# Moving the fold of three batches out of the recurrent part and reordering the last units of a fused mLSTM, soft-MoE and MLP kernel

## The chip, the core and the metric

The kernel runs on one core of a Trainium2 chip. The metric is the device time in microseconds; the median over runs is compared. The engines are TensorE (PE; its weight loads are listed apart as PEld), VectorE (DVE), ScalarE (ACT), GpSimd (POOL) and SyncE (SP), whose queue issues the transfers.

## What is computed

Three layers in a row: a matrix LSTM with exponential gates over 4 x 8 heads of 768 steps and width 40, a soft mixture of 8 experts with 4 slots each, and an MLP with a squared ReLU.

```python
def _attn_ref(q, k, v, i_gate, f_gate, o_gate):
    ...
        m_new = np.maximum(f_gate[:, :, t] + m, i_gate[:, :, t])
        C = f_stab[:, :, None, None] * C + i_stab[:, :, None, None] * np.einsum('bhd,bhe->bhde', vt, kt)
        n = f_stab[:, :, None] * n + i_stab[:, :, None] * kt
        ...
        y[:, :, t] = o * h_tilde / denom

def _moe_ref(x, phi, w1, w2):
    logits = x @ phi
    d = softmax of logits over the tokens; c = softmax of logits over the slots
    slot_input = d.T @ x
    for e in range(E):
        h = np.maximum(slot_input[e] @ w1[e], 0.0)
        slot_out[e] = h @ w2[e]
    return c @ slot_out

def _moe2_ref(x, w_in, w_out):
    g = np.maximum(x @ w_in, 0.0) ** 2
    return g @ w_out
```

(The softmax lines are shortened to words.)

## The kernel before

The recurrence is cut into chunks of 128 steps and groups of three heads (the last group has two): 11 groups of 6 chunks are the `units` of the main loop. A unit has products for the decay mask (`e_mb`, L440), for the scores q k (`e_st`, L471), for the state's update (`e_u`, L499), for what the earlier chunks give (`e_inter`, L544) and for the chunk itself (`e_av`, L559). VectorE multiplies scores and mask to `p` (`e_pm`, L483), updates the state (`e_uc`: `cu` at L518), and GpSimd masks it (`e_mask`, `cbd` at L534); `e_num` (tmp at L581, num at L588) and `fin` or `fin_last` (L611 to L653) make the outputs x in SBUF.

The order on each engine is the order in which the code is written: nothing reschedules it. Work for the mixture is put between the units by generators: `filler` is called once or twice in a unit with a string of tags, and each tag (P for transposes on TensorE, N, D and n for VectorE, A for ScalarE, G and g for GpSimd, Q for the logits) lets waiting generators take a step. One of them is `merge`, which brings the three finished batches' slot sums xs3 to one common maximum and folds them into one group of 32 rows: the product `xs3 x cb3` at L798, three products of two passes each, in the bank ps_lt, copied to xs4[96:128] at L804. Another is `merge_tr`, which transposes the outputs of the last batch (`moe_kt`, L675, kt = 0 and 1) and takes the logits (L684).

Behind the loop stands straight code for the last batch. The third part of the outputs is transposed (kt2, L1054) and copied (L1056), its logits are taken, and the maximum follows: nmx (L1066), mxr (L1070), a product for the row maximum (L1072). `tr_el` transposes the exponentials, and VectorE copies them to `en` (L1080, L1081). The slot sums `xx` (L1096) are combined with the folded batches (L1109 to L1114) to the experts' inputs. Then come the experts' layers: `ffn_up(0)` and `ffn_up(1)` (L1148), `relu` (L1153, scaled by rt128, L1172 and L1173), the transposes `ffn_tr` (L1200) and `ffn_down` (L1219). Weights of the experts stream in meanwhile.

In between stand two side tasks. `cbuild(tg)` prepares the combine weights of 512 tokens: its first step casts and subtracts on VectorE (chl, L1015 and L1016), its second transposes four times on TensorE into a bank of the tag o or m (L1022), its third copies on ScalarE (cst, L1027); `cgo(a, b)` takes the next step of a and of b. `wo_narrow(f)` rebuilds a part of the MLP's output weights: two passes on ScalarE (L140, L144) and two on VectorE (L148, L152). `warm(n)` puts n bf16 products in a place where TensorE waits (L197).

PSUM has two banks each of the tags mb, st and o, one of m, and ps_lt; a tag's banks are taken in turn, so a writer waits for whatever still reads the bank's former tile. From 186 us on the MLP runs over the tokens (L1344 and L1416).

Of the kernel before, what the change touches and what calls it, by code (L numbers as in the profile page):

```python
# [20 lines left out]
END = "PADNngG"  # L21
# [22 lines left out]
def kernel(  # L44
# [446 lines left out]
    def e_u(g, c):  # L491
        nh = groups[g][1]
        nd, nv = nh * D, nh * DV
        n = units.index((g, c)) + 2
        t = bank("st")
        if n < NU:
            stk[units[n]] = t
        u = t[:, 384:512]
        nc.tensor.matmul(  # L499
            u[0:nd, 0:nv],  # L500
            lhsT=kin[g][:, c].rearrange("p n d -> p (n d)"),
            rhs=wvs.pop((g, c)).rearrange("p n d -> p (n d)"),
            start=True,
            stop=True,
        )
        us[g, c] = u

    def e_uc(g, c):
        nh = groups[g][1]
        nd, nv = nh * D, nh * DV  # L510
        uv = us.pop((g, c))[0:nd, 0:nv].rearrange("p (n d) -> p n d", d=DV)
        hv = hm[0:nd, 0:nh].unsqueeze(2).to_broadcast([nd, nh, DV])
        cb = cb01[g, c % 2] if g < 2 else wk.tile([120, nh, DV], F32, tag="cbd", name="cbd", bufs=2)
        if c == 0:
            nc.vector.tensor_tensor(out=cb[0:nd], in0=uv, in1=hv, op=ALU.mult)
        else:
            cu = wk.tile([120, nh, DV], F32, tag="cu", name="cu", bufs=1)
            nc.vector.scalar_tensor_tensor(  # L518
                out=cu[0:nd],
                in0=cbds[g, c - 1][0:nd],  # L520
                scalar=dec120[0:nd, g, c : c + 1],
                in1=uv,
                op0=ALU.mult,
                op1=ALU.add,
            )
            masks.append((cb[0:nd], cu[0:nd], hv))
        cbds[g, c] = cb
# [235 lines left out]
    def merge():  # L763
# [30 lines left out]
        yield "P"  # L794
        t = ltb
        nc.tensor.matmul(t[:, DM : DM + B1], lhsT=sel4f[0:96], rhs=tt3, start=True, stop=True)
        for b in range(B1):
            nc.tensor.matmul(  # L798
                t[96:128, 0:DM], lhsT=cb3[:, b, :], rhs=xs3[:, b, :], start=(b == 0), stop=(b == B1 - 1)
            )  # L800
        yield "N"
        nc.vector.tensor_reduce(out=se4[96:128], in_=t[96:128, DM : DM + B1], axis=AX.X, op=ALU.add)
        yield "A"
        nc.scalar.copy(xs4[96:128], t[96:128, 0:DM])  # L804

    def merge_tr():
        yield from moe_kt(B - 1, 0)
        yield from moe_kt(B - 1, 1)
        yield "Q", {"merge"}
        logits(range(2))  # L810

# [74 lines left out]
    for i, (g, c) in enumerate(units):  # L886
# [73 lines left out]
        elif i > 1 and nm:  # L960
            finish(nm)
            g1, c1 = units[i - 2]
            if c1 == NC - 1:
                add(fin(g1), ("fin", g1), [("sig", b) for b in batches(g1)])
        elif g == NG - 1 and c > 1:
            f1 = fin(g, c - 3, c - 1)
            if c == 3:
                add(f1, ("fin", g), [("sig", B1)])
            else:
                for _ in range(3):  # L970
                    next(f1)
        if i >= QI:
            advance("Q", 1)
        filler(END, i >= LI, i < 20)
    xf = xb[B - 2].rearrange("p c d -> p (c d)")
    hsb = xf[:, 0:FF]
    sT01 = xf[:, FF : FF + 64 * NE].rearrange("p (k w) -> p k w", k=2)
# [7 lines left out]
    while fillers:  # L985
        advance("W")
        filler("QPNADngG")
    while w2s:
        ld_w2(*w2s.pop(0))
    pl.close()  # L990
# [43 lines left out]
    def cgo(*tgs):  # L1034
        for tg in tgs:
            next(cbs[tg], None)
# [5 lines left out]
    for n in (4, 5):  # L1042
        ld_w2(w2p[n], *w2o[2 + n])
    load_wo(wo0, 0, 4)
    dumt = bank("mb")
    cgo(0, 1)
    warm(WT[6], dumt)
    x3 = xb[B1]
    k0, kn = KT[2]
    xT = xTs[2]  # L1050
    for blk in (range(0, 4), range(4, 6)):
        t = bank("o")
        for n, c in enumerate(blk):
            nc.tensor.transpose(t[0:kn, 128 * n : 128 * n + 128], x3[:, c, k0 : k0 + kn], ident)  # L1054
        w = 128 * len(blk)
        nc.scalar.copy(xT[0:kn, 128 * blk[0] : 128 * blk[0] + w], t[0:kn, 0:w])  # L1056
        warm(WT[5], dumt)
    logits([2])
    load_wo(xTw[:, 0 : SLOT // 2], 6, 2)
    cgo(0)  # L1060
    warm(WT[0], dumt)
    el_ = mp.tile([128, 2, TQ], F32, tag="el", name="el")
    el = el_[0:96]
    en = mp.tile([128, 2, 2, 96], F32, tag="en", name="en")
# [7 lines left out]
    nc.tensor.matmul(tm[:, 0:4], lhsT=sel4f, rhs=mxr, start=True, stop=True)  # L1072
    rm = ca.tile([128, 1], F32, name="rm")
    nc.vector.tensor_reduce(out=rm, in_=tm[:, 0:4], axis=AX.X, op=ALU.max, negate=True)
    warm(WT[1], dumt)

    def tr_el(m):
        t = bank("mb" if m == 0 else "o")
# [9 lines left out]
    nc.vector.tensor_scalar(out=comb, in0=selF, scalar1=es, scalar2=None, op0=ALU.mult)  # L1088
    tt = ca.tile([128, 1], F32, name="tt")
    nc.vector.tensor_tensor(out=tt, in0=es, in1=se4, op=ALU.mult)  # L1090
    cgo(0, 1, 2)
    warm(WT[2], dumt)
    xx = bank("st")
    for u in range(2):
        for r in range(NQ):
# [6 lines left out]
            )  # L1102
    nc.scalar.copy(xs4[0:96, 0:128], xx[0:96, 0:128])
    nc.vector.tensor_copy(xs4[0:96, 128:DM], xx[0:96, 128:DM])
    cgo(1, 2, 3)
    warm(WT[3], dumt)
    t = bank("st")
    for kt in range(2):
        nc.tensor.matmul(  # L1109
# [16 lines left out]
    load_wo(x3.rearrange("p c d -> p (c d)")[:, 0 : SLOT // 2], 4, 2)  # L1126
    for n in (6, 7):
        ld_w2(w2p[n], *w2o[2 + n])
    cgo(3)
    warm(WT[4], dumt)  # L1130
    NP = NE // 2
    ys = {}

# [25 lines left out]
    for n in range(4):  # L1159
        for r in range(2):  # L1160
            nc.vector.tensor_copy(
                repm[32 * n : 32 * n + 32, 64 + 128 * n + 32 * r : 96 + 128 * n + 32 * r],
                ident[32 * n : 32 * n + 32, 32 * n : 32 * n + 32],
            )
    finish(wo_narrow(0, *par_t))
    cgo(2, 3)
    for h in range(2):
        nc.gpsimd.memset(hT[:, 4 * h : 4 * h + 4], 0.0)
    for n in range(6):
# [37 lines left out]
        )  # L1207

    ffn_up(1, range(0, 3))
    ffn_tr(0)  # L1210
    ffn_up(1, range(3, 5))
    relu(1)
    so = bank("st")
# [14 lines left out]
    next(n4)  # L1228
    next(n4)
    ffn_down(0)  # L1230
    ffn_tr(1)
    next(cl)
    finish(n4)
    finish(cl)
# [283 lines left out]
```

## Time and profile before

| | us |
|---|---|
| median of 3 runs | 387.26 (387.14 to 388.26) |
| the profiled execution | 386.97 |
| its span | 385.2 |
| TensorE busy | 374.2 |
| VectorE busy | 264.1 |
| ScalarE busy | 254.0 |
| GpSimd busy | 102.9 |

Times in the views count from the start of the span. The recurrence with its fillers takes until about 152 us, the mixture's last part until 182, the MLP the rest. The view of stages lists for each stretch the busy time of every engine, the granted clock (PEclk, 1.00 is the upper level) and the mean share of the DMA engines. The chain is followed back from the last instruction: each piece is what held up the end at that time. The timelines list groups of one engine, line and tile, with the idle time ahead of them and what ended it.

### The profile page before, as it was taken

The numbers are of one execution on the slowest core, as the hardware profiler recorded it, in microseconds if no ns is written. First come the engines' busy times: TensorE is split into PE (matmuls) and PEld (weight loads), VectorE is DVE, ScalarE is ACT, GpSimd is POOL, SyncE is SP. The second block draws the span as 40 slices with busy tenths as digits, with TensorE's granted clock in tenths as the row PEclk, the third lists the DMA queues.
The fourth block names the chain that finished last, engine by engine and source line by source line (L and its number), as shares of the span: only waits on it lengthen the run. The fifth ranks groups of instructions, "written<-read, shape, count | busy, mean of one in ns | idle before, by whom it ended". The sixth has DMA issues, their size and how long they took to land.

```text
span 385.2 us, 9124 instructions
## 1 busy us (share of the span) xinstructions
PE 374.2 (97%) x3420; PEld 333.4 (87%) x3420; DVE 264.1 (69%) x602; ACT 254.0 (66%) x579; POOL 102.9 (27%) x208
## 2 busy tenths in 40 slices
PE   8899999999899999999999999999999999999996
PEld 6789998889879886435699899999999999999996
DVE  7868889878988577738688865555555555555551
ACT  7798776569656752544697976676676667657652
POOL 4665976766677546000000000000000000000000
PEclk9999999999999999999999999999999999999999
DMA  5886897899969786999000010020010001002001
GB/s 174 280 299 207 282 314 235 260 325 344 305 185 386 212 324 195 361 378 381 2 3 0 2 68 3 0 70 0 3 66 4 1 2 68 2 1 70 1 2 68
DMA packets 19541, 56.62 MB, mean 147 GB/s; under 512 B 2481, under 2 KB 7561, under 8 KB 19113
## 3 DMA queue, kind: packets, MB, share of 16 engines
q1 hardware_dynamic: 19497, 56.04, 42.7%
q8 instruction: 27, 0.44, 0.5%
q14 instruction: 17, 0.14, 0.1%
HBM read 52.10 MB, written 3.93 MB: 145 GB/s over the span
## 4 chain that ended last, share of the span: by engine, by line
PE 79%; DVE 8%; POOL 5%; ACT 3%; issue 3%; SPq 1%; DMA 0%; POOLq 0%; DVEq 0%; ACTq 0%
PE ps_mb L1416 18%; PE ps_st L1416 17%; PE ps_lt L1416 9%; PE ps_st L471 7%; PE ps_o L1344 4%; PE ps_o L559 4%; PE ps_o L544 3%; PE ps_st L1219 2%; DVE p L483 2%; PE ps_m L1344 2%; PE ps_st L499 2%; PE ps_lt L684 2%; POOL w L461 2%; PE ps_mb L440 1%; DVE x L631 1%
## 5 line engine op out<-in xcount | busy, mean ns | idle before, releaser
L1367 DVE CAST hi<-ring 128x512 fp32r<-128x512 f32 x93 | 39.7, 427 | 61.2 <-ACT ring L1366 53.0
L1368 DVE TENSOR_TENSOR lo<-ring,hi 128x512 fp32r<-128x512 f32 x96 | 66.5, 692 | 9.8
L454 ACT ACTIVATE w<-ps_mb,qt 128x128 f32<-128x128 f32 x192 | 56.5, 367 | 17.2 <-PE ps_mb L440 10.1
L1349 ACT ACTIVATE ring<-ps_o 128x512 f32<-128x512 f32 x64 | 38.3, 598 | 34.2 <-PE ps_o L1344 34.2
L1366 ACT ACTIVATE ring<-ring 128x512 f32<-128x512 f32 x93 | 58.8, 633 | 3.0
L471 PE MATMUL ps_st<-par 120*128 120x128 f32 (+1 forms) x384 | 56.9, 284 | 0.1
L1416 PE MATMUL ps_mb<-wohlh,hi 128*128 128x320 f32 x160 | 49.5, 310 | 0.0
L1416 PE MATMUL ps_mb<-wohlh,lo 128*128 128x320 f32 x160 | 49.4, 310 | 0.0
L1416 PE MATMUL ps_mb<-wohll,hi 128*128 128x320 f32 x160 | 49.3, 309 | 0.0
L471 PEld LDWEIGHTS ps_st<-par 120*128 120x128 f32 (+1 forms) x384 | 47.9, 192 | 0.3 <-issue 0.3
L1416 PE MATMUL ps_st<-wohll,hi 128*128 128x320 f32 x144 | 44.7, 310 | 0.0
L1416 PE MATMUL ps_st<-wohlh,hi 128*128 128x320 f32 x144 | 44.7, 310 | 0.0
L1416 PE MATMUL ps_st<-wohlh,lo 128*128 128x320 f32 x144 | 44.6, 310 | 0.0
L461 POOL TENSOR_SCALAR_AFFINE_SELECT w<-w 128x384 f32<-128x384 f32 (+1 forms) x66 | 37.1, 562 | 17.8 <-ACT w L454 12.1
L483 DVE TENSOR_TENSOR p<-ps_st,w 128x384 f32<-128x384 f32 (+1 forms) x66 | 35.5, 538 | 4.7 <-POOL w L461 3.7
L1416 PEld LDWEIGHTS ps_mb<-wohll,hi 128*128 128x128 f32 x160 | 30.0, 188 | 1.4
L1349 ACT ACTIVATE ring<-ps_m 128x512 f32<-128x512 f32 x32 | 19.1, 598 | 18.4 <-PE ps_m L1344 18.4
L1416 PEld LDWEIGHTS ps_mb<-wohlh,hi 128*128 128x128 f32 x160 | 30.1, 188 | 0.0
L1416 PEld LDWEIGHTS ps_mb<-wohlh,lo 128*128 128x128 f32 x160 | 30.1, 188 | 0.0
L559 PE MATMUL ps_o<-par,p 128*64 128x41 f32 x768 | 29.0, 232 | 0.0
L1416 PEld LDWEIGHTS ps_st<-wohll,hi 128*128 128x128 f32 x144 | 27.1, 188 | 2.0 <-issue 0.6
L559 PEld LDWEIGHTS ps_o<-par,p 128*64 128x64 f32 x768 | 25.1, 138 | 4.0 <-issue 0.2
(275 smaller groups left out, 772.0 us busy)
## 6 DMA issues: line engine op xcount, KB each, us to landing
ring<-in_w_dram SPq DMA_DIRECT2D x22, 640.0 KB
stage<-in_w_in_dram SPq DMA_DIRECT2D x10, 512.0 KB
par<-in_w_dram SPq DMA_DIRECT2D x6, 640.0 KB
out_dram<-ring SPq DMA_DIRECT2D x24, 160.0 KB
par<-in_v_s_dram SPq DMA_DIRECT2D x9, 369.0 KB
par<-in_k_s_dram SPq DMA_DIRECT2D x9, 360.0 KB
x<-in_o_gate_dram SPq DMA_DIRECT2D x9, 320.0 KB
par<-in_k_t_dram SPq DMA_DIRECT2D x23, 120.0 KB
```

What stands on the lines that cost most here:

```text
L454: nc.scalar.activation(w[:, j, :], mb[:, 128 * j : 128 * j + 128], AF.Exp, bias=qt3[:, c, h0 + j : h0 + j + 1])
L461: nc.gpsimd.affine_select(out=w, in_=w, pattern=[[0, nh], [1, 128]], compare_op=ALU.is_ge, fill=0.0, base=0, channel_multiplier=-1)
L471: nc.tensor.matmul(st[:, 128 * j : 128 * j + 128], lhsT=kbd[g % 2][0:nd, j, ts_], rhs=qin[g][0:nd, ts_], start=True, stop=True,)
L483: nc.vector.tensor_tensor(out=p, in0=sts.pop((g, c))[:, 0 : nh * 128].rearrange("p (n t) -> p n t", n=nh), in1=ws.pop((g, c)), op=ALU.mult,)
L544: nc.tensor.matmul(pos[g, c // 2][:, o0 : o0 + nv], lhsT=qin[g][0:nd, 128 * c : 128 * c + 128], rhs=cbds[g, c - 1][0:nd], start=True, stop ...
L559: nc.tensor.matmul(po[t0 : t0 + 64, o0 : o0 + DV], lhsT=p[:, j, t0 : t0 + 64], rhs=vin[g][:, c, j, :], start=True, stop=True,)
L1344: nc.tensor.matmul(t, lhsT=gst[n][:, 128 * k : 128 * k + 128], rhs=cst[tg], start=True, stop=True)
L1349: nc.scalar.activation(r, t, AF.Relu)
L1366: nc.scalar.activation(r, r, AF.Square)
L1367: nc.vector.tensor_copy(hi, r)
L1368: eng.tensor_tensor(out=lo, in0=r, in1=hi.bitcast(F32), op=ALU.subtract)
L1416: nc.tensor.matmul(acc[u][:, 0:DM], lhsT=l_[:, 128 * u : 128 * u + 128], rhs=wohl[r_, f // 8][:, f % 8, :], start=(f == 0 and a == 0), sto ...
```

## The change

It does this:

- `merge` no longer folds; a generator `fold` holds the three products, now in a bank of the tag st, and takes them one by one: one behind the kt2 transposes, one behind the logits of kt2, one behind tr_el. The copy to xs4[96:128] follows the last one.
- The keep-warm products of this part (`warm(WT[...])`) go.
- The update products of the last units c = 3 and 4 take a bank of the tag mb rather than sharing a st bank, and for the last three units VectorE both masks and adds (`e_uc`) in place of VectorE and then GpSimd.
- `fin` of the last group comes one unit earlier, and the fillers of the last two units are cut, so that the transposes of kt = 0 and 1 stand behind the last unit's products.
- The second copy of kt2 is VectorE's.
- The steps of `cbuild` are put at other places: chl(0) to chl(3) are each transposed later than before.

```diff
 def e_u(g, c):
-        t = bank("st")
-        if n < NU:
+        t = bank("st" if n < NU - 1 else "mb")
+        if n < NU - 1:
             stk[units[n]] = t
 ...
 def e_uc(g, c):
+            if units.index((g, c)) >= NU - 3:
+                nc.vector.tensor_tensor(out=cu[0:nd], in0=uv, in1=hv, op=ALU.mult)
+                nc.vector.scalar_tensor_tensor(
+                    out=cb[0:nd],
+                    in0=cbds[g, c - 1][0:nd],
+                    scalar=dec120[0:nd, g, c : c + 1],
+                    in1=cu[0:nd],
+                    op0=ALU.mult,
+                    op1=ALU.add,
+                )
+                cbds[g, c] = cb
+                return
 ...
 def merge():
         nc.tensor.matmul(t[:, DM : DM + B1], lhsT=sel4f[0:96], rhs=tt3, start=True, stop=True)
+        folds.append(cb3)
+        yield "N"
+        nc.vector.tensor_reduce(out=se4[96:128], in_=t[96:128, DM : DM + B1], axis=AX.X, op=ALU.add)
+
+    folds = []
+
+    def fold():
+        t = bank("st")
         for b in range(B1):
             nc.tensor.matmul(
-                t[96:128, 0:DM], lhsT=cb3[:, b, :], rhs=xs3[:, b, :], start=(b == 0), stop=(b == B1 - 1)
-            )
-        yield "N"
-        nc.vector.tensor_reduce(out=se4[96:128], in_=t[96:128, DM : DM + B1], axis=AX.X, op=ALU.add)
-        yield "A"
+                t[96:128, 0:DM], lhsT=folds[0][:, b, :], rhs=xs3[:, b, :], start=(b == 0), stop=(b == B1 - 1)
+            )
+            if b < B1 - 1:
+                yield
         nc.scalar.copy(xs4[96:128], t[96:128, 0:DM])
+        yield
 
     def merge_tr():
         yield from moe_kt(B - 1, 0)
-        yield from moe_kt(B - 1, 1)
+        yield from moe_kt(B - 1, 1, ("m", "mb"))
 ...
-        elif g == NG - 1 and c > 1:
-            f1 = fin(g, c - 3, c - 1)
-            if c == 3:
+        if g == NG - 1 and c in (2, 4):
+            finish(nm or ())
+            nm = None
+            f1 = fin(g, c - 2, c)
+            if c == 2:
                 add(f1, ("fin", g), [("sig", B1)])
 ...
-        filler(END, i >= LI, i < 20)
+        filler(END if i < NU - 2 else "ADngG" if i == NU - 2 else "", i >= LI, i < 20)
 ...
+    fd = fold()
 ...
-    dumt = bank("mb")
-    cgo(0, 1)
-    warm(WT[6], dumt)
 ...
-        nc.scalar.copy(xT[0:kn, 128 * blk[0] : 128 * blk[0] + w], t[0:kn, 0:w])
-        warm(WT[5], dumt)
+        (nc.vector.tensor_copy if blk[0] else nc.scalar.copy)(
+            xT[0:kn, 128 * blk[0] : 128 * blk[0] + w], t[0:kn, 0:w]
+        )
+    next(fd)
+    cgo(0)
     logits([2])
     load_wo(xTw[:, 0 : SLOT // 2], 6, 2)
-    cgo(0)
-    warm(WT[0], dumt)
+    next(fd)
 ...
-    warm(WT[1], dumt)
 ...
-    cgo(0, 1, 2)
-    warm(WT[2], dumt)
+    next(fd)
     xx = bank("st")
 ...
-    cgo(1, 2, 3)
-    warm(WT[3], dumt)
+    cgo(0, 1)
 ...
-    cgo(3)
-    warm(WT[4], dumt)
+    cgo(1, 0)
 ...
+    cgo(1, 2)
     finish(wo_narrow(0, *par_t))
-    cgo(2, 3)
+    cgo(3)
 ...
     ffn_up(1, range(0, 3))
+    cgo(2)
     ffn_tr(0)
+    cgo(2)
     ffn_up(1, range(3, 5))
 ...
     ffn_down(0)
+    cgo(3)
     ffn_tr(1)
+    cgo(3)
```

How the instructions of two engines stand now, at the three places that matter. First TensorE in the last two units, before (L798 the fold, L499 the update, L471 scores, L559 the chunk itself, L544 inter-chunk, L675 kt = 0 and 1, L684 logits):

```order
L798 MATMUL ps_lt<-xs_111,cb_2588 32x320 x3
L499 MATMUL ps_st<-wv,par_70 80x82
L471 MATMUL ps_st<-par_70 128x128 x2
L559 MATMUL ps_o<-par_70,p 64x41 x8
L544 MATMUL ps_o<-cbd,par_70 128x82
...
L675 MATMUL ps_m<-ident,x 120x128 x4
...
L675 MATMUL ps_m<-ident,x 120x128 x2
L684 MATMUL ps_lt<-xTw,phs 32x256 x6
```

and after (L556 is now the inter-chunk product, L571 the chunk itself, L687 kt = 0 and 1, L696 the logits, L1074 the transposes of kt2, L818 a fold product):

```order
L499 MATMUL ps_mb<-wv,par_70 80x82
L556 MATMUL ps_o<-cbd,par_70 128x82
L571 MATMUL ps_o<-par_70,p 64x41 x8
L556 MATMUL ps_o<-cbd,par_70 128x82
L687 MATMUL ps_m<-ident,x 120x128 x4
L687 MATMUL ps_mb<-ident,x 120x128 x2
L696 MATMUL ps_lt<-xTw,phs 32x256 x6
L1074 MATMUL ps_o<-ident,x 80x128 x6
L818 MATMUL ps_st<-xs_111,cb_2588 32x320
L696 MATMUL ps_lt<-xTw,phs 32x256 x3
```

The fold is gone from ahead of the two last updates and stands, in single products, between kt2 and its logits and further on; the kt transposes stand behind the last inter-chunk product. Next TensorE through the experts' first layer, before (L1148 ffn_up, L1172 rt, L1080 tr_el(1), L1200 ffn_tr, L1219 ffn_down):

```order
L1148 MATMUL ps_st<-ring,x 32x512 x20
L1172 MATMUL ps_m<-rt,selJ 128x1
L1080 MATMUL ps_o<-ident,el 128x96 x2
L1148 MATMUL ps_o<-ring_84,x 32x512 x12
L1200 MATMUL ps_mb<-ident,x 128x128 x4
L1148 MATMUL ps_o<-ring_84,x 32x512 x8
L1219 MATMUL ps_st<-stage,ring 32x320 x8
```

and after (L1166 ffn_up, L1191 rt, L1101 tr_el(1), L1045 the transposes of chl, here chl(2), L1219 ffn_tr, L1240 ffn_down):

```order
L1166 MATMUL ps_st<-ring,x 32x512 x20
L1191 MATMUL ps_m<-rt,selJ 128x1
L1101 MATMUL ps_o<-ident,el 128x96 x2
L1166 MATMUL ps_o<-ring_84,x 32x512 x12
L1045 MATMUL ps_o<-ident,chl 128x128 x4
L1219 MATMUL ps_mb<-ident,x 128x128 x4
L1166 MATMUL ps_o<-ring_84,x 32x512 x8
L1240 MATMUL ps_st<-stage,ring 32x320 x8
```

Four transposes of chl into a bank of the tag o have come in behind the twelfth product of ffn_up(1); another four, of chl(3), follow ffn_down(0). The o banks are taken in turn, and the tile before chl(2)'s in its bank is that of tr_el(1). Last VectorE at the same time, before (L148 and L152 wo_narrow, L1173 rt128, L1081 the copy of tr_el(1) to en):

```order
L148 SCALAR_TENSOR_TENSOR par_71<-wo_2726,par_71 128x640
L152 SCALAR_TENSOR_TENSOR wo_2726<-par_70,par_71 128x640
L1173 COPY rt_2690<-ps_m 128x1
L148 SCALAR_TENSOR_TENSOR par_71<-wo_2726,par_71 128x640
L152 SCALAR_TENSOR_TENSOR wo_2726<-par_70,par_71 128x640
L1081 COPY en<-ps_o 128x192
```

and after (L1038 and L1039 cast and subtract chl, of chl(2) and then of chl(3); L1192 rt128, L1102 the copy to en):

```order
L1038 CAST chl<-call 128x8x32
L1039 TENSOR_TENSOR chl<-call,chl 128x8x32
L148 SCALAR_TENSOR_TENSOR par_71<-wo_2723,par_71 128x640
L152 SCALAR_TENSOR_TENSOR wo_2723<-par_70,par_71 128x640
L1038 CAST chl<-call 128x8x32
L1039 TENSOR_TENSOR chl<-call,chl 128x8x32
L1192 COPY rt_2677<-ps_m 128x1
L148 SCALAR_TENSOR_TENSOR par_71<-wo_2723,par_71 128x640
L152 SCALAR_TENSOR_TENSOR wo_2723<-par_70,par_71 128x640
L1102 COPY en<-ps_o 128x192
```

The casts of chl(2) and chl(3) have come in ahead of rt128; the copy to en stands at its old place behind the second wo_narrow.

## Rows read from the trace of the kernel before

**Rows 1.** The page: busy time of each engine, and shares of the chain.

```profile
PE 374.2 (97%) x3420; PEld 333.4 (87%) x3420; DVE 264.1 (69%) x602; ACT 254.0 (66%) x579; POOL 102.9 (27%) x208
...
PE 79%; DVE 8%; POOL 5%; ACT 3%; issue 3%; SPq 1%; DMA 0%; POOLq 0%; DVEq 0%; ACTq 0%
```

**Rows 2.** Stages: stretch, length, busy by engine, clock, DMA share, GB/s.

```profile
152.70:160.80 8.10, 7.67 (x66) 4.94 (x69) 5.71 (x23) 4.61 (x12) 0.28 (x1) 1.00 0.96 340
160.80:180.30 19.50, 19.50 (x221) 7.64 (x221) 12.58 (x34) 8.56 (x15) 1.90 (x2) 1.00 0.99 393
```

**Rows 3.** The chain in the last units: start, length, what.

```profile
145.43 1.73 PE ps_lt L798 x6
...
150.00 0.44 PE ps_m L675 x4
...
151.04 0.38 PE ps_o L544 x2
```

**Rows 4.** Timeline of the same stretch: start, length, group, idle ahead and releaser.

```profile
146.11 0.54 POOL L534 TENSOR_TENSOR cbd<-cu,hm 80x82 f32<-80x82 f32 x1
...
148.27 0.41 DVE L483 TENSOR_TENSOR p<-ps_st,w 128x256 f32<-128x256 f32 x1
...
148.60 0.71 DVE L631 SCALAR_TENSOR_TENSOR x<-x,numr 128x240 f32<-128x240 f32 x2
...
149.53 0.30 DVE L518 SCALAR_TENSOR_TENSOR cu<-cbd,dec,ps_st 80x82 f32<-80x82 f32 x1 [0.21 <-POOL cbd L534]
...
149.55 0.45 PE L544 MATMUL ps_o<-cbd,par 80*128 80x82 f32 x2 [0.48 <-POOL cbd L534]
...
149.75 0.32 DVE L581 TENSOR_TENSOR tmp<-ps_o,qt 128x164 f32<-128x164 f32 x1
...
151.46 0.33 DVE L581 TENSOR_TENSOR tmp<-ps_o,qt 128x164 f32<-128x164 f32 x1
...
153.25 0.33 DVE L653 TENSOR_TENSOR x<-x,rcl 128x160 f32<-128x160 f32 x1
```

**Rows 5.** The chain from the end of the logits to the experts.

```profile
152.72 0.54 PE ps_mb L197 x4
...
154.37 0.91 PE ps_lt L684 x6
...
155.30 0.43 DVE nmx L1066
...
156.83 0.44 PE ps_o L1022 x4
...
158.56 0.59 PE ps_o L1022 x4
```

**Rows 6.** The chain in the experts' first layer.

```profile
160.80 4.43 PE ps_st L1148 x40
...
165.85 2.71 PE ps_o L1148 x24
```

**Rows 7.** Timeline of VectorE beside it, and two chl passes ahead of it.

```profile
159.21 0.28 DVE L1015 CAST chl<-call 128x256 fp32r<-128x256 f32 x1
159.52 0.43 DVE L1016 TENSOR_TENSOR chl<-call,chl 128x256 fp32r<-128x256 f32 x1
...
163.65 0.82 DVE L152 SCALAR_TENSOR_TENSOR wo<-par,par 128x640 int32<-128x640 int32 x1
165.57 0.16 DVE L1173 COPY rt<-ps_m 128x1 f32<-128x1 f32 x1 [1.10 <-PE ps_m L1172]
167.91 0.82 DVE L148 SCALAR_TENSOR_TENSOR par<-wo,par 128x640 int32<-128x640 int32 x1 [2.18 <-ACT par L144]
...
169.51 0.35 DVE L1081 COPY en<-ps_o 128x192 f32<-128x192 f32 x1
```

**Rows 8.** Timeline of ScalarE in that stretch: relu(0) and the second pass of f = 2.

```profile
165.77 0.69 ACT L1153 ACTIVATE x<-ps_st,rt 128x512 f32<-128x512 f32 x1 [4.04 <-DVE rt L1173]
...
167.06 0.82 ACT L144 ACTIVATE par<-wo 128x640 int32<-128x640 uint16 x1
```

## The prediction

> **What bounds the kernel now.** I read the page first: TensorE is busy for 374.2 us of the span [rows 1], and the chain that ended last is TensorE for 79% of it. So an engine other than TensorE counts only where TensorE stands still for it, and the time moves by what TensorE gains or loses in the stretch that the change touches, 145 to 172 us. Behind it the kernel is TensorE's to the end, and a shift at 180 us is a shift of the end. Next I read the stages: from 152.7 to 160.8 us TensorE is busy 7.67 of 8.10 us, and from 160.8 to 180.3 it has no gap at all, 19.50 of 19.50 [rows 2]. That divides the change in two. In the first part there are waits in which something can be hidden, and in the second whatever is added costs its whole length. Then I read the chain and the timelines around the pieces that move.
>
> **The fold and the last units: the lead.** The fold leaves a place where it stood on the chain with 1.73 us [rows 3]; it would have cost nothing only if TensorE had been waiting there. Its removal does not bring the rest forward by 1.73, because VectorE then sets the pace. The starting point is the same in both kernels: the masked state of the unit before is ready when GpSimd's L534 at 146.11 ends, 146.65 [rows 4]. From there VectorE works in a row in the changed kernel: mask and state update (two passes like the 0.30 of 149.53, 0.58), p 0.41, the two output passes of L631 0.71, a reciprocal 0.15, mask and update for the last state 0.55, then tmp, num and one output pass 1.02 (0.32 to 0.33 each and gaps), which gives 150.07 for the tmp of the last unit [rows 4]. From that tmp to the last output pass the trace has 151.46 to 153.58, 2.12 us, so the outputs are complete at 152.19, where they were at 153.58 [rows 4]: a lead of 1.39. TensorE itself could be at the last inter-chunk product at 148.4 (151.04 less the fold's 1.73, the 0.44 of the kt1 transposes that now stand behind it [rows 3], and the 0.48 that TensorE waited for GpSimd's mask [rows 4]) and waits there until about 149.1. So of the 2.2 us set free, 0.7 turn into a new wait for VectorE.
>
> Behind that the last two kt2 transposes end at about 152.45. The second copy is now VectorE's, beside ScalarE's first, and it hides under the first fold product (1.73/3 = 0.58), so the logits of kt2 start at 153.03. They started at 154.37 [rows 5]: lead 1.34. The second fold product lies in the wait for the maximum: that starts with nmx, 155.30 before and 153.98 now, and the row-maximum product is issued 0.92 behind it, so 0.58 are hidden. The third lies behind tr_el, in the wait for the copy of en; the two transposes end 1.53 us behind nmx's start (155.30 to 156.83 [rows 5]), at 155.49, the product ends at 156.07, and en's copy (0.36) is earlier than that. The slot sums xx then start at 156.07 where they started at 157.28: lead **1.21**. From there to the ffn lie two blocks of four chl transposes in both kernels, now chl(0) and chl(1) where it was chl(2) and chl(3), so the 3.52 from 157.28 to 160.80 stay. So ffn_up(0) starts at 159.59, where the trace has 160.80 [rows 5, 6].
>
> The seven keep-warm products that go (four of them are the 0.54 at 152.72 [rows 5]) lay in waits: removing them gives nothing, as their successor waited for the outputs anyway. The swap of mask and update from GpSimd to VectorE is in the sum above; the one-unit-earlier pass of fin sits on VectorE and GpSimd ahead of it. SP's queue keeps its order.
>
> **What it adds behind the ffn's start.** chl(0) stood before in the wait for the maximum and chl(1) at 156.83 in the wait for en's copy [rows 5], so neither cost anything. Since all move back by two places, two blocks of four transposes, chl(2) and chl(3), now stand inside the ffn, where TensorE has no gap [rows 2]. Each costs 0.59, the row at 158.56 [rows 5]: **1.18**. Nothing there can take them in: what they stand ahead of are transposes and products whose operands are ready.
>
> **The new wait.** chl(2)'s transposes write an "o" bank, and the previous user of that bank is tr_el(1), whose result VectorE copies to en. In the order VectorE copies it behind both narrowing passes of f = 2, which wait for ScalarE's two, which queue behind relu(0), which waits for rt128. Before, that copy starts at 169.51 and ends at 169.86 [rows 7], the links being rt128 at 165.57, relu 165.77, ScalarE's L140 and L144 (the second at 167.06), VectorE's L148 at 167.91 with the 2.18 idle ahead of it [rows 7, 8]. From rt128's start to the copy's end it is 4.29 us, and nobody on TensorE waits for it there. In the changed kernel TensorE arrives at chl(2) at 159.59 + 4.43 (ffn_up(0)) + 0.62 (rt and tr_el) + 2.71 (twelve products of ffn_up(1) [rows 6]) = 167.35. VectorE: narrow(0) ended at 164.47 before [rows 7]; it now has chl(2)'s cast and subtraction (0.28 and 0.43 at 159.21, 0.74 with the gap [rows 7]) ahead of it and the lead of 1.21, so 164.00, and chl(3)'s 0.74 behind it, so rt128 is copied at 164.74. Without chl(3) it would be 159.59 + 4.77 = 164.36, so 0.38 of the delay are chl(3)'s. The copy ends at 164.74 + 4.29 = 169.03, the transposes start at 169.07: a wait of **1.72** on TensorE, with all of the ffn queued behind it.
>
> **Sum.** -1.21 + 1.72 + 1.18 = +1.69 us. The profiled execution took 386.97, so 388.66; the median of the runs is 0.29 above that execution, so 388.95, given as 388.9. Bounds: the lead lies between 0.7 (nothing hidden of the first and third fold product, less a little) and 2.2 (the fold and GpSimd's wait, with no new wait); the wait between 0 and 1.72; the two blocks between 0.9 (0.44 each, the shortest of their kind, at 156.83 [rows 5]) and 1.2. The weight stream does not set the time: its share of the DMA engines is 0.99 from 160.8 to 180.3 [rows 2], which would matter if TensorE came to ffn_down earlier; it comes later.
>
> **Rivals.** First, the wait or VectorE's chain is shorter: if the last state is ready when TensorE arrives, the lead is 1.9, and if chl(3) finds VectorE idle ahead of rt128, the wait is 1.34; then +0.6, 387.9, and with one of the two +1.0 to +1.3. For it speaks that VectorE's passes overlap in the trace (p at 148.27 is 0.41 long and the next starts at 148.60 [rows 4]), so that a sum of nine of them may be some tenths too long. Within 0.3% of before, about what can be told from no change here, are 386.1 to 388.4.
>
> Second, on the other side: the bank is free when TensorE arrives. That is decided by one point, whether en's copy ends before 167.35. If VectorE took it ahead of the narrowing passes, at 165.9 as soon as the transposes end, the wait is gone and with it 1.72: 387.2, and 386.2 if the whole 2.2 of lead come through. Against it stands VectorE's order, which is fixed as written, with the copy last.
>
> Third, the clock. The granted clock is 1.00, TensorE's upper level of 2.4 GHz, in all three stages [rows 2], gaps up to half a microsecond included. The change takes the keep-warm products out and leaves waits of 0.7, 0.7 and 1.7 us. If the clock fell to 1.2 GHz in the long one, what follows up to ffn_down (two blocks of four transposes at 0.59, eight products at 2.71/12 each: 3.0 us [rows 5, 6]) takes twice as long: +4.7 in all, 391.9. No gap of this length before a fall is among the rows, and the products on either side of it are dense, so I give it little. The Trainium skill, "TensorE: Matmul & The Clock Gate", Part 4 (PE-mode transpose), says that transposes do not count as busy for the clock as products do; by that the wait, with four chl and four ffn transposes behind it, is a longer quiet stretch than it looks, and it speaks for this rival; no row here shows a fall by which that could be tried.
>
> That the change does not do what it says: the fold could come to stand on the chain again. At worst the first and third product cost their 0.58 in full; the first costs 0.3 of it in the sum above already.
>
> **How the numbers follow.** The forecast, wait and blocks outweigh the lead, 388.2 to 389.8: 0.60. The first rival, 387.5 to 388.2: 0.21. The second, 386.0 to 387.3: 0.10. The clock: 0.09. The range of 387.2 to 390.1 leaves out most of the second and the clock. Slower by over 0.3% (above 388.4) are most of the forecast and the clock: 0.68. Faster by over 0.3% takes the second rival with all of its lead: 0.06. The rest, 0.26, is within.
>
> **What would show it.** In the profile after: the fold in pieces of 0.58 with no 1.73 on the chain; no wait for GpSimd's cbd; a wait of about 0.7 at the last inter-chunk product for VectorE; ffn_up(0) starting at 159.6; one wait of chl(2)'s transposes for VectorE's copy of en, 1.3 to 1.8 long; the two blocks of 0.59 on the chain inside the ffn; ffn_down ending near 182.0 where it was 180.3; clock 1.00 throughout. It is wrong if ffn_up(0) starts before 159.0, or if the wait for en is under 0.7: then the first or second rival holds.

## The result and the profile after

The changed kernel takes 392.62 us (median of 4, 392.32 to 392.72); the kernel before, run beside it, 387.76 (387.14 to 388.33). The ratio is 1.0124, with an interval of 1.0103 to 1.0146. It is slower, as forecast, but by 4.9 us, and the forecast was 1.7. The time lies outside the range, just above the price of the third rival (the clock, 391.9), which had been given 0.09. Two of the four executions of the kernel before took 387.1 to 387.3 and two 388.3, so the loss is 5.4 against the first pair and 4.3 against the second.

The page, as [rows 1] did for the kernel before: TensorE's busy time has grown by 1.6 us, though it has 7 fewer products.

```profile
span 390.6 us, 9112 instructions
...
PE 375.8 (96%) x3413; PEld 335.0 (86%) x3413; DVE 266.6 (68%) x605; ACT 254.2 (65%) x578; POOL 101.3 (26%) x206
```

The stages of the changed kernel (stretch, length, busy time of PE, PEld, DVE, ACT and POOL, granted clock, DMA share, GB/s). The column to read is the granted clock. It was 1.00 in both stretches of [rows 2], and also ahead of them, in the last units of the kernel before:

```profile
148.00:151.00 3.00, 2.52 (x43) 2.10 (x43) 2.21 (x8) 0.57 (x3) 2.00 (x4) 1.00 0.73 212
```

After the change:

```profile
144.00:148.00 4.00, 2.81 (x32) 2.37 (x32) 3.87 (x15) 0.95 (x4) 3.48 (x8) 0.94 0.52 142
148.00:151.00 3.00, 3.00 (x25) 2.75 (x26) 2.81 (x12) 0.21 (x1) 0.73 (x3) 0.50 0.85 345
151.00:154.00 3.00, 3.00 (x19) 1.42 (x18) 1.48 (x7) 0.86 (x2) 0.99 (x2) 0.50 0.92 290
154.00:158.00 4.00, 3.06 (x23) 1.42 (x24) 2.58 (x10) 1.69 (x5) 0.00 (x0) 0.96 1.00 415
...
166.00:170.00 4.00, 3.12 (x27) 0.88 (x27) 1.81 (x5) 2.09 (x3) 0.00 (x0) 1.00 0.93 332
170.00:174.00 4.00, 2.65 (x12) 1.77 (x16) 1.97 (x5) 0.61 (x2) 0.00 (x0) 0.67 1.01 416
174.00:178.00 4.00, 4.00 (x44) 1.71 (x40) 0.00 (x0) 2.15 (x4) 0.00 (x0) 0.90 0.64 260
```

TensorE fell to its lower level, 1.2 GHz, twice: from 147.5 to past 154 us, and from 171.5 to past 174. The first fall begins inside the wait for VectorE's cbd (147.11 to 147.83); behind it TensorE was busy in every microsecond from 148 to 154 (3.00 of 3.00), and yet at half its clock, so that the same work takes longer and fills the time. The waits of TensorE from 140 to 186 us:

```profile
PE ps_o L1045 <- DVE en L1102: 2.2, 1, 2.2
PE ps_m L1094 <- DVE mxr L1092: 0.9, 1, 0.9
PE ps_o L556 <- DVE cbd L520: 0.7, 1, 0.7
PE ps_o L556 <- POOL cbd L546: 0.5, 1, 0.5
```

The wait for VectorE's cbd is there at 0.7, as the sum had it, and the wait of chl(2) for en, at 2.2 instead of 1.72. Two things are not as foreseen: one wait of 0.5 for GpSimd's cbd is left, ahead of the units whose masks moved, and the wait for mxr is 0.9 where the kernel before has 0.3, since chl(0) no longer stands in it. The timeline of TensorE shows the two falls in single groups: the logits of kt = 0 and 1, ffn_up(0) and the wait for en.

```profile
147.83 0.69 PE L556 MATMUL ps_o<-cbd,par 80*128 80x82 f32 x2 [0.72 <-DVE cbd L520]
...
151.42 1.93 PE L696 MATMUL ps_lt<-xTw,phs 120*32 120x256 f32 x12
...
161.28 4.50 PE L1166 MATMUL ps_st<-ring,x 128*32 128x512 f32 x40
...
171.35 1.11 PE L1045 MATMUL ps_o<-ident,chl 128*128 128x128 f32 x4 [2.23 <-DVE en L1102]
```

The same view of the kernel before has these logits and ffn_up(0) as:

```profile
151.57 1.15 PE L684 MATMUL ps_lt<-xTw,phs 120*32 120x256 f32 x12
...
160.73 4.50 PE L1148 MATMUL ps_st<-ring,x 128*32 128x512 f32 x40
```

And the chain behind that wait, where [rows 6] had the ffn without a gap:

```profile
171.35 1.11 PE ps_o L1045 x4
172.46 0.85 PE ps_mb L1219 x4
173.31 2.60 PE ps_o L1166 x16
175.91 1.08 PE ps_st L1240 x16
176.99 0.59 PE ps_o L1045 x4
```

The account against the profile before: ffn_up(0) starts at 161.28 where the same view has 160.73 (the chain of [rows 6] says 160.80), 0.55 later and not 1.21 earlier; the wait for en is 2.23; two blocks of chl transposes at 0.59 are 1.18; and the second fall stretches chl(2), ffn_tr(0) and the eight products to 4.56 us (1.11 + 0.85 + 2.60) from 3.03, which is 1.53. The transposes behind them take 0.44 where they took 0.59, which gives back 0.15. That is 5.34. The span grew by 5.4 (390.6 less 385.2).

### The profile page after: what moved, and what is told of

The parts are those of the page before. It is cut to its first block, busy times and chain, and to the rows that moved or that the text cites. A ratio compares the mean times of both kernels' runs of the same rounds, so it can differ in the third digit from the quotient of the medians.

```text
span 390.6 us, 9112 instructions
## 1 busy us (share of the span) xinstructions
PE 375.8 (96%) x3413; PEld 335.0 (86%) x3413; DVE 266.6 (68%) x605; ACT 254.2 (65%) x578; POOL 101.3 (26%) x206
## 4 chain that ended last, share of the span: by engine, by line
PE 55%; DVE 1%; ACT 1%; issue 0%
PE ps_mb L1439 18%; PE ps_st L1439 16%; PE ps_lt L1439 9%; PE ps_o L1367 4%; PE ps_st L1240 2%; PE ps_m L1367 2%; PE ps_o L1166 1%; PE ps_o L1045 1%; PE ps_m L1323 0%; PE ps_mb L1219 0%; PE ps_st L1337 0%; PE ps_mb L1323 0%; DVE par L148 0%; DVE wo L152 0%; PE ps_st L1338 0%; DVE wohll L1278 0%
## 5 line engine op out<-in xcount | busy, mean ns | idle before, releaser
L471 PE MATMUL ps_st<-par 120*128 120x128 f32 (+1 forms) x384 | 56.9, 284 | 0.9 <-DMA par<-in_q_t_dram 0.9
L471 PEld LDWEIGHTS ps_st<-par 120*128 120x128 f32 (+1 forms) x384 | 47.9, 191 | 1.1 <-DVE ring L367 1.1
L571 PE MATMUL ps_o<-par,p 128*64 128x41 f32 x768 | 29.4, 233 | 0.0
L571 PEld LDWEIGHTS ps_o<-par,p 128*64 128x64 f32 x768 | 25.4, 139 | 4.0
```

The source lines that it names most:

```text
L471: nc.tensor.matmul(st[:, 128 * j : 128 * j + 128], lhsT=kbd[g % 2][0:nd, j, ts_], rhs=qin[g][0:nd, ts_], start=True, stop=True,)
L571: nc.tensor.matmul(po[t0 : t0 + 64, o0 : o0 + DV], lhsT=p[:, j, t0 : t0 + 64], rhs=vin[g][:, c, j, :], start=True, stop=True,)
```

## The experiments

Each was run beside the kernel before. In the code, `...` stands for lines or arguments left out. The mean granted clock of every execution is recorded. By the profiled ones, a fall of 6.8 us shows in it as about 0.991, one of half that length as 0.994 to 0.996, both, or a single fall of 10 us, as 0.986 or 0.987, and none as 0.998 to 1.000. Where no profile was taken, the falls are read from this mean. Of the kernel before's executions beside these experiments 84 of 97 were at 0.998 or more, with medians between 386.8 and 387.0 us on four chips, 11 at 0.994 to 0.996 and 2 lower. So for each experiment two things can be read: the time where the clock held, and how often there was a long fall (0.992 or less).

**en copied first.** The wait and the second fall, taken away together.

```diff
-    finish(wo_narrow(2, *par_t))
     tr_el(1)
+    finish(wo_narrow(2, *par_t))
```

> The changed kernel with one pair of statements swapped: tr_el(1) with its copy to en stands ahead of wo_narrow(2), so VectorE frees the bank of chl(2) before the narrowing. Theory (the wait for en is new, and the fall of the clock at 171.5 us comes from that wait): the wait of 2.23 us goes, and with it the 1.53 us that the two blocks of transposes and eight products lost at the lower clock; 3.7 us less, about 388.9, clock 1.00 from 155 us on. Rival (the transposes that now stand in the ffn bring the clock down by themselves): the wait goes, the fall stays, 2.2 us less, about 390.4.

Measured: 388.56 us, ratio 1.0038 (1.0024 to 1.0052). The profile has no wait for en, and from 158 us on the clock is 1.00; the first fall is as before, and the ten executions are at 0.987 to 0.991. The theory's 388.9 and its one fall less are met, so here the second fall goes with the wait and not with the transposes. The stages of 148 and of 170 us:

```profile
148.00:151.00 3.00, 3.00 (x25) 2.75 (x26) 2.81 (x12) 0.21 (x1) 0.69 (x2) 0.50 0.88 362
...
170.00:174.00 4.00, 4.00 (x43) 1.84 (x41) 1.80 (x4) 2.49 (x5) 0.00 (x0) 1.00 1.01 417
```

**Keep-warm products in the waits of the last units.**

```diff
+        if i >= NU - 2:
+            warm(6 if i == NU - 2 else 6)
         e_inter(g, c)
```

> The changed kernel with six bf16 products of 128x256 put ahead of each of the last two inter-chunk products, in the waits for VectorE's cbd. Theory (the clock falls at 147.5 us because TensorE stands still there while the fold is gone): clock 1.00 through 144 to 156 us, ffn_up(0) starts about 1.7 us earlier, at 159.6, and the time is about 390.9, with the later wait and its fall as they were. Rival (what is missing is the fold's dense products, and a few products in a wait don't stand for them): the clock still falls between 147 and 150 us, time 392.3 to 392.9.

Measured: 391.05 us, ratio 1.0091 (1.0059 to 1.0124), near the theory's 390.9 but not for its reason. In the profile the clock fell at 147 us all the same, ahead of the first of these products (147.53), though TensorE had waited for nothing since 144.8, and came back at 150.4, almost four microseconds earlier than without:

```profile
146.00:147.00 1.00, 1.00 (x20) 0.78 (x19) 0.90 (x5) 0.21 (x1) 1.00 (x3) 1.00 0.00 0
147.00:148.00 1.00, 1.00 (x7) 0.87 (x8) 0.96 (x3) 0.00 (x0) 0.93 (x3) 0.51 0.99 97
```

So the fall does not need the wait for cbd. One execution of four held the clock throughout (1.000) and took 389.5: that is 2.6 above the kernel before, and the only time of the whole change at full clock. The sum with the measured wait gives 2.20 (-1.21 + 2.23 + 1.18), with these products not counted. In the profiled execution the products went with a shorter fall and did not prevent it.

**The fold alone moved.** The kernel before with next(fd) at the three new places and nothing else.

```diff
 def merge():
-        for b in range(B1):
-            nc.tensor.matmul(t[96:128, 0:DM], lhsT=cb3[:, b, :], rhs=xs3[:, b, :], ...)
+        folds.append(cb3)
 ...
+    next(fd)
     logits([2])
 ...
+    next(fd)
     cgo(0)
 ...
+    next(fd)
     cgo(0, 1, 2)
```

> The kernel before with the fold alone moved: three products one by one behind kt2, behind its logits and behind tr_el; keep-warm products, masks, order of the units and chl all as before. Theory (the fold's 1.73 us of products held the clock up in the last units): the granted clock falls between 147 and 150 us also here, the lead of 1.2 us is eaten, time 387.3 to 389.5. Rival (the clock falls only because of the wait for VectorE's masks): clock 1.00 throughout, and the lead is seen, about 386.4.

Measured: 389.0 us, ratio 1.0031 (0.9991 to 1.0071), and this mean hides what matters. Two executions held the clock (mean 1.000) and took 385.82 and 386.08; four lost it once (0.990 and 0.991) and took 388.9 to 389.1; four at 0.986 took 390.3 to 390.6, and the profiled one of these has a second, short fall near the start of the program, where nothing is changed. So moving the fold does give a lead where the clock holds: 1.0 us under the kernel before (386.94 at held clock on that chip), on two executions. And moving it by itself brings a long fall in 8 executions of 10; where that is the only fall, it costs 3.0 us. Here masks, order of units, chl and keep-warm products are all as before. The stages of the profiled execution:

```profile
144.00:148.00 4.00, 3.53 (x42) 3.04 (x39) 3.79 (x19) 2.13 (x9) 2.77 (x7) 1.00 0.55 220
148.00:151.00 3.00, 2.24 (x16) 1.75 (x17) 2.36 (x9) 0.17 (x1) 2.36 (x6) 0.73 0.96 304
151.00:154.00 3.00, 3.00 (x29) 2.01 (x30) 1.75 (x8) 0.90 (x3) 1.25 (x3) 0.50 0.64 167
154.00:158.00 4.00, 4.00 (x28) 2.06 (x22) 1.90 (x8) 0.85 (x2) 0.02 (x1) 0.73 0.93 381
```

**The places of chl alone.** The kernel before with the diff's `cgo` lines only.

> The kernel before with the places of cbuild's steps alone changed, chl(2) behind the twelfth product of ffn_up(1) and chl(3) behind ffn_down(0); fold, masks and keep-warm products as before. Theory (this part alone brings two blocks of 0.59, a wait for en of 1.7 to 2.3 and a fall of the clock behind it): 4.4 to 5.0 us slower than before, about 392.4, clock 0.50 for some 3 us from about 172 us on. Rival (the wait is there, but the clock falls only after the first fall has been through): 2.9 to 3.4 slower, about 390.9.

Measured: 391.7 us, ratio 1.0122 (1.0089 to 1.0156): this part alone costs as much as the whole change. The waits from 140 to 186 us:

```profile
PE ps_o L1022 <- DVE en L1080: 2.2, 1, 2.2
PE ps_o L544 <- POOL cbd L534: 1.0, 2, 0.5
PE ps_m L1071 <- DVE mxr L1069: 0.8, 1, 0.8
PE ps_st L1094 <- DVE en L1080: 0.5, 1, 0.5
```

The wait for en is there, but in this execution the clock did not fall behind it (1.00 from 162 us on, against the theory); it fell at 158, behind the waits for mxr and en which chl(0) and chl(1) had filled before:

```profile
158.00:162.00 4.00, 4.00 (x25) 2.40 (x20) 1.02 (x4) 0.85 (x2) 0.00 (x0) 0.57 0.72 231
...
157.85 2.15 PE L1094 MATMUL ps_st<-x,en 128*32 128x320 f32 x12 [0.45 <-DVE en L1080]
```

So chl(0) and chl(1) were not free to move: they cost nothing where they stood, and without them waits of 0.8 and 0.5 stand open, with a fall behind them. From the inter-chunk product ahead of the fold to ffn_up(0) it is 17.5 us here (145.18 to 162.68) and 16.1 in the kernel before. The open waits are not what costs: up to the slot sums xx (157.85 here, 157.28 before) it is 12.67 us against 12.61. From xx to ffn_up(0), at the lower clock, it is 4.83 against 3.45. Three executions are at 0.995, one at 0.986.

**The fold in the waits of the last units.** The changed kernel, en first, the fold's products ahead of the last two inter-chunk products and behind kt2.

```diff
+        if i >= NU - 2:
+            next(fd)
         e_inter(g, c)
 ...
```

> The changed kernel with en copied ahead of wo_narrow(2) and the fold's three products at other places: one ahead of each of the last two inter-chunk products, in the waits for VectorE's cbd, and the third behind kt2. Theory (the lead of 1.2 us is there as long as TensorE has dense products between 144 and 148 us; the fall of the clock takes it): clock 1.00 in nearly all executions, lead 1.2 to 1.6 us, less the two blocks of chl transposes (1.18) in the ffn: 386.4 to 387.2, within 0.3% of before. Rival (the clock falls because of the waits and the short products of the last units, whatever stands in the waits): clock 0.50 from about 148 to 154 us as with en first alone, about 388.5.

Measured: 388.64 us, ratio 1.0048 (1.0029 to 1.0068). The rival holds: the clock falls at 147.5 in the profile, and the mean clocks are 0.986 to 0.996, never higher, four of seven with a long fall. The first product stands at 147.2 now, 1.8 us behind the fold's old start, and there it did not keep the clock, which fell while TensorE was busy with it:

```profile
147.00:147.50 0.50, 0.50 (x6) 0.26 (x4) 0.50 (x1) 0.00 (x0) 0.50 (x2) 1.00 0.68 154
147.50:148.00 0.50, 0.50 (x2) 0.00 (x0) 0.50 (x2) 0.00 (x0) 0.25 (x1) 0.54 0.95 266
```

**Fold in the waits, chl at its old places.** The same units, and behind the logits as the kernel before (the second copy of kt2 stays VectorE's, and four keep-warm products stand ahead of kt2).

> As the kernel before from the logits on (chl transposes at their old places, in waits ahead of the ffn; en copied where it was; four keep-warm products ahead of kt2), with the changed kernel's last units, and the fold's products in the waits for cbd and behind kt2. Theory (lead about 1.4 us, nothing added inside the ffn, no wait for en, clock held): 385.2 to 386.0, faster than both kernels by over 0.3%. Rival (the clock falls in the last units also with the fold there): 387.5 to 389.

Measured: 387.95 us, ratio 1.0024 (1.0004 to 1.0043). Three executions of twelve at 0.998 or more took 386.4 to 386.8, the others 387.7 to 389.6, four of them with a long fall. Faster than the changed kernel, not than the one before. Also where the clock held it misses 385.2 to 386.0: the profile shows mxr late (a wait of 0.7), since the casts of chl(0) and chl(1) now lie ahead of nmx on VectorE with the second copy of kt2.

**No keep-warm products.** `WT = (0, 0, 0, 0, 0, 0, 0)` in the kernel before.

> The kernel before with the seven keep-warm products between 152 and 156 us left out and nothing else. Theory (they lay in waits, and the fold's products are what holds the clock): time and clock as before within 0.3%. Rival (the missing keep-warm products are what lets the clock fall in the changed kernel): clock 0.50 for some us behind 150 us, 1.5 to 3.5 us slower.

Measured: 387.0 us, ratio 1.0008 (0.9993 to 1.0024). Six of ten executions are at 0.999 or more, four at 0.994 to 0.996 with 388.1 to 388.4, none has a long fall. Within 0.3%, as expected: they cost nothing, and without them there may be more short falls (4 of 10 against 11 of 97). With the fold in its place, their absence does not bring a long fall.

**Clearing hT on ScalarE.** Why the wait was 2.23 and not 1.72.

```diff
-        nc.gpsimd.memset(hT[:, 4 * h : 4 * h + 4], 0.0)
+        nc.scalar.activation(
+            hT[:, 4 * h : 4 * h + 4].rearrange("p f w -> p (f w)"),
+            ident[:, 0:1].to_broadcast([128, 1024]),
+            AF.Copy,
+            scale=0.0,
+        )
```

> The changed kernel with the two clearings of hT moved from GpSimd (0.95 us each, the first beside VectorE's cast of chl(2)) to ScalarE, which is idle there. Theory (that cast took 1.07 us where others take 0.28 because GpSimd cleared at the same time, and so made the wait for en 2.23 where the sum gave 1.72): the cast takes 0.28 to 0.3, the wait 1.4 to 1.7, the time 0.5 to 0.9 less, 391.5 to 392.1; both falls of the clock stay. Rival (the cast is slow for another reason): cast about 1.07, wait 2.2, time as the changed kernel's.

Measured: 389.9 us, ratio 1.0074 (1.0052 to 1.0096). First VectorE's cast of chl(2) and GpSimd's clearing in the changed kernel:

```profile
163.30 0.95 POOL L1187 MEMSET ring<- 128x1024 f32 x1 [11.31 <-PE ps_st L1166]
163.32 1.07 DVE L1038 CAST chl<-call 128x256 fp32r<-128x256 f32 x1
```

and here the same cast, and the wait:

```profile
164.08 0.29 DVE L1038 CAST chl<-call 128x256 fp32r<-128x256 f32 x1
```

```profile
PE ps_o L1045 <- DVE en L1102: 1.5, 1, 1.5
```

The cast is back at 0.29 and the wait at 1.46. The time came down by more than the 0.5 to 0.9 expected, because the second fall went too: no execution was at 0.987 or lower any more, and in the profile the clock is 1.00 behind the wait. That the length of the wait decides whether the clock goes with it is suggested by these four executions and not shown: in the chl order alone a wait of 2.22 had none behind it.

**The fold undone.** The changed kernel, en first, with the fold back in its row in merge.

> The changed kernel with en copied first, and the fold undone: its three products stand in a row in merge again, ahead of the last two updates. Theory (the fold's 1.73 us of products keep the clock up, and the fall costs as much as moving it saves): clock 1.00 in most executions, as in the kernel before; the lead is gone, the two chl blocks of 0.59 in the ffn stay, so 387.7 to 388.4, about what en first alone takes at the lower clock (388.6). Rival (masks on VectorE and the order of the last units let the clock fall also with the fold there): mean clock 0.99 and 390 or more.

Measured: 388.73 us, ratio 1.0048 (1.0030 to 1.0066): neither expectation. With the fold in its place the clock holds through the last units, where it had fallen; it falls later, at 158 in the profile, behind the waits for mxr (1.1) and en (0.5) that the change empties of chl:

```profile
148.00:151.00 3.00, 2.93 (x46) 2.40 (x42) 2.74 (x11) 0.58 (x2) 0.70 (x2) 1.00 0.80 242
151.00:154.00 3.00, 2.72 (x23) 1.03 (x18) 2.32 (x10) 1.07 (x3) 1.03 (x2) 1.00 1.04 432
154.00:158.00 4.00, 2.50 (x22) 1.06 (x19) 2.00 (x8) 1.20 (x5) 0.00 (x0) 0.99 0.99 406
158.00:162.00 4.00, 4.00 (x22) 2.98 (x24) 2.39 (x12) 1.41 (x4) 0.00 (x0) 0.50 0.87 293
```

**How much of the fold.** Three kernels from the kernel before: two of the fold's products in TensorE's wait for GpSimd's mask and the third behind kt2; one of the three moved; two moved.

> The kernel before with two of the fold's products moved into TensorE's wait for GpSimd's mask (ahead of the inter-chunk product of the last but one unit), the third behind kt2. Theory (moved later and into a wait they save 0.9 to 1.1 us where the clock holds, and the clock falls in most executions because 145 to 147 us is left without them): executions at mean clock 1.00 take 385.8 to 386.1, the others 387.5 to 389. Rival (placed there they hold the clock): all at 1.00, 385.8 to 386.1.

> The kernel before with the last of the fold's three products moved behind kt2 and two left in their place. Theory (what holds the clock is the amount of products there): the clock holds nearly as often as before, 0.3 to 0.6 us saved, 386.2 to 386.6. Rival (the whole fold is needed): most executions at 0.99, 388 or more.

> The kernel before with one of the fold's products left in its place, one moved behind kt2 and one behind tr_el. Theory: between the kernel before and the fold moved whole: executions at mean clock 1.00 take 386.0 to 386.3, and a part of them, less than the 8 of 10 of the whole move, lose the clock and take 388 to 389.5. Rival (one product is as good as three for the clock): all at 1.00.

Measured: 389.32 us (ratio 1.0046, 1.0015 to 1.0078), 387.39 (1.0009, 1.0000 to 1.0019) and 387.59 (1.0024, 1.0008 to 1.0041). Executions with a long fall: with no product in place 8 of 10 (fold alone moved) and 5 of 10 (in GpSimd's wait), with one 3 of 12, with two none of 12, with all three 2 of 97. The savings are not to be seen with one and two moved: where the clock held, they took 387.3 and 387.5 (387.0 before; in GpSimd's wait 386.3 to 387.0). In these edits the fold kept its bank, ps_lt, and the logits there wait 0.5 us for ScalarE's copy of the fold, or the fold for the copy of el (0.6). That wait is my edit's. In the profile of the fold in GpSimd's wait a single fall lasts from 147.3 to 157.7 us.

**The new units with the fold in place.** The changed kernel's last units; fold, and all behind the logits, as before, but for four of the seven keep-warm products, which are left out.

> The changed kernel's last units (masks on VectorE, update products in mb banks, fin earlier, kt = 0 and 1 behind the last product) with the fold left in its row in merge and everything behind the logits as in the kernel before, three keep-warm products instead of seven. Theory (with the fold in place and the chl transposes in their waits TensorE is never left long with short work, so the clock holds; VectorE's masks save GpSimd's wait of 0.48 and bring the outputs forward): logits of kt2 0.6 to 0.9 us earlier than before, executions at mean clock 0.998 or more as frequent as before (about 9 of 10), 386.0 to 386.5. Rival (the new order of the units lets the clock fall by itself, whatever the fold does): most executions below 0.996, 387.5 to 389.

Measured: 386.42 us, ratio 0.9990 (0.9975 to 1.0005). Nine of twelve executions are at 0.998 or more, with 385.8 to 386.8, and none has a long fall. The logits of kt2 start at 153.64, 0.73 earlier than before. The units' new order does not lose the clock:

```profile
148.00:151.00 3.00, 2.94 (x49) 2.51 (x49) 2.90 (x11) 0.34 (x2) 0.57 (x2) 1.00 0.75 213
151.00:154.00 3.00, 2.89 (x25) 1.21 (x24) 2.60 (x11) 1.68 (x4) 1.15 (x3) 1.00 1.02 416
154.00:158.00 4.00, 3.72 (x32) 1.95 (x29) 2.73 (x11) 1.59 (x5) 0.00 (x0) 1.00 1.02 429
```

**The masks alone.** The kernel before with the diff's `e_u` and `e_uc`.

> The kernel before with one part of the change alone: mask and update of the last three units both on VectorE, with their update products in mb banks. Theory: the wait of 0.48 for GpSimd's mask goes, VectorE has two more passes ahead of p; 0.2 to 0.5 us saved, 386.4 to 386.8, clock as before. Rival (VectorE is the later engine there): no gain, within 0.2 us of before, with a wait for VectorE's cbd in the place of GpSimd's.

Measured: 386.46 us, ratio 0.9989 (0.9978 to 1.0000), eleven of twelve executions at 0.999 or more. The second wait for GpSimd's mask is gone and none for VectorE's has come. This version and the one above, which are not told apart, are what the runs point to: this one is 0.4 to 0.7 us under the kernel before, at the edge of what can be told, and about 1.3% under the changed kernel by the two ratios.

## Why the prediction was wrong

**Right: the direction, and three of the terms.** The wait of 0.7 for VectorE's masks (0.72), the two blocks of chl transposes on the ffn (0.59 each at full clock), and the wait for en with its place and its cause. Its size came out at 2.23 instead of 1.72. The cast of chl(2) was priced at 0.28 by a row without GpSimd beside it and took 1.07; with GpSimd's clearing moved away the wait was 1.46, so the rest of that chain was some 0.26 shorter than summed.

**Not seen: the lead of 1.21.** It is a sum of steps each at full clock. Parts of it are there where the clock held: 1.0 with the fold alone moved (two executions), 0.5 with the units alone (median 386.3 against 386.8). The whole of it was not measured apart at full clock. In the changed kernel it became a loss of 0.55, which is 1.76 off. The step that failed is the one in which the fold's removal was costed: I asked what the fold held up and what would be late next, and took every row that follows at its duration in the kernel before; in the sum the clock stood at nothing. The logits of kt = 0 and 1 alone took 1.93 instead of 1.15, twice four transposes and eight products later 1.5 more.

**Wrong: the weight and the place of the clock.** The third rival had the mechanism, and its 391.9 is the nearest of the prices, but by accident: it put one fall of 3.0 us behind the wait for en (measured 1.53 there) and none at the fold, where the larger one was (1.76, if the sum's lead is right). Two readings led there. The first was that gaps up to half a microsecond at clock 1.00 show the clock to be safe, and that "the products on either side of it are dense". (The prediction says three stages; [rows 2] shows two, and the last units are not among them.) The gap there grew by little, from 0.48 to 0.72; what went was the 1.73 us of products in a row, in a stretch that otherwise consists of transposes and products of 41 to 128 columns, with their weight loads. Nor is a stretch without a gap for that reason safe: in the profiles of the keep-warm products and of the fold in the waits the clock fell at 147.0 and 147.5 with TensorE busy. The second was that of what goes only the keep-warm products were looked at for the clock. They were nearly without effect. With the whole fold in place and the chl transposes in their waits there was a long fall in 2 of 131 executions (the kernel before, no keep-warm products, the units, the masks); with the fold alone moved in 8 of 10, and with the chl order alone all four had a fall, one of them long. The page that the prediction cited, the Trainium skill's "TensorE: Matmul & The Clock Gate", Part 4, on transposes not counting as busy like products, fits the busy and yet slow stretch from 148 to 154, of which transposes fill some 2.1 us (L687 and L1074); that chl transposes in a wait nonetheless made a difference (the chl order alone, and the fold undone) is not what one would read from it, though there the wait around them also grew.

**The rivals.** A free bank (the second) was ruled out by the order, and the wait was there. A shorter wait (the first) did not come.

What stays open: why the same kernel loses the clock in one execution and not in the next. The runs give the frequencies, not the reason. Nor did any run put other dense products where the fold had stood: moving the fold takes products out of that place and also brings what follows forward, and the runs do not part the two.

## What to carry to other kernels

Work that stands on the critical engine's chain can be paying for the clock of what follows it: before moving dense products out of a stretch of short ones, price the stretch at half the clock as well, and give that case a weight to match. Read the mean clock of every execution, not only the median time: a median between two levels hides both a real gain and how often it is lost. And before moving filler out of a wait that it hides in, count the wait that it leaves open and the place it goes to: four transposes that cost nothing cost 0.59 in a stretch without gaps, and there their bank brought a wait of 2.2.

## What the runs showed of the hardware

A cast on VectorE from f32 to fp32r took 1.07 us beside a GpSimd clearing of 0.95 and 0.28 to 0.29 without it; the passes with two tensor inputs beside GpSimd's second clearing kept their 0.82. The Trainium skill, "GPSIMD Engine Reference", section 8 (Key points), says that GpSimd shares its SBUF interfaces with VectorE, with contention for VectorE instructions in a 2-port mode or with two inputs from SBUF. The slow cast fits this if it runs in such a mode, which no row shows; the passes with two inputs were not slowed by this clearing, which writes and has no input.

The clock came back by itself in the same stretch of work: in the fold's experiment it rose to 1.00 before 158 us, in the changed kernel before 155, under logits and the transposes of kt2. One long fall cost 3.0 us with the fold alone moved (388.9 against 386.0 at held clock) and 2.2 with two of its products moved (389.6 against 387.5), so a mean clock of 0.991 is the sign of some 0.6 to 0.8% of the time.
